# Second layer's output product in four of six token blocks: seven products of halves in place of eight for two of three output chunks

## The chip, the cores and the metric

The kernel runs on one core of one Trainium2 chip. Times are device microseconds (us) of one execution. Engines are named as the profile names them: PE is TensorE's matmuls, PEld its weight loads, DVE is VectorE, ACT is ScalarE, POOL is GpSimd, and SP is the queue that issues the DMAs.

## The reference

```python
def _attn_ref(q, k, v, beta):            # a delta-rule recurrence over 768 steps, 4 x 8 heads of 48
    ...
def _moe_ref(x, w_in, w_out):            # first layer
    h = x @ w_in
    g = np.maximum(h, 0.0) + np.log1p(np.exp(-np.abs(h)))
    return (g @ w_out).astype(np.float32)

def _moe2_ref(x, w_in, w_out):           # second layer: the change is in its g @ w_out
    h = x @ w_in
    g = h * np.cos(h)
    return (g @ w_out).astype(np.float32)

x = np.ascontiguousarray(attn_out.transpose(0, 2, 1, 3)).reshape(B * S, H * D)   # 3072 x 384
x = _moe_ref(x=x, **moe_kwargs)          # w_in 384 x 2048, w_out 2048 x 384
return _moe2_ref(x=x, **moe2_kwargs)
```

## The kernel before

The attention recurrence runs in 24 steps of 128 tokens (4 batches of 32). The first layer follows it in blocks of 256 tokens and fills PE between the recurrence's steps; the second layer runs in `NB2` = 6 blocks of 512 tokens after it, and its first blocks overlap the first layer's end. Every float32 matrix product is made of three float16 matmuls, on the high and low halves of both operands (`PAIRS`: high by high, high by low, low by high), which add up in one PSUM bank.

In the second layer (`ph` = 1) a block `j` goes through the 16 slices of 128 hidden units (`u` = `f`). `moe_in` makes the slice's h: nine matmuls (3 chunks of 128 inputs by 3 halves), each of 512 token columns, into one of five PSUM banks (psH0, psH1, psC0, psC1, psY; `hring`). Then comes a chain of operations of 128x512: on DVE an add that rounds (L918) and a subtraction (`stt`, L415), on ACT Abs and Sin (`actf`, L420 and L422), on DVE the product that gives g (L415), on ACT a copy to float16, the high half (`copy`, L399), and on POOL or DVE a subtraction that leaves the low half (`tt`, L411). `moe_out` then makes, for each of the three chunks of 128 outputs, three matmuls of 512 columns that add into that chunk's accumulator bank (accA, accB and psA; `acc2`). It comes two slices behind `moe_in`. `moe_end` copies the three accumulators to SBUF (`xs`, which lies in `w0`), and three DMAs store them.

The order of instructions is not the order of the code. Each call of `put` records an operation with the engines that it may run on, its estimated duration and the keys that it reads and writes, and `Plan.run` works out an order for each engine from these estimates. Its decisions are fixed in the built program: every engine runs its own list in order, and waits on semaphores for the others. For the `base` of a second-layer matmul the planner takes `moe_left`, the matmul time that is still to come.

Weights come as float32; `conv` splits each slice into float16 halves (`v`, one tile for two slices; L481 the high half, L489 the low half) while the first layer ends.

Of the kernel before, what the change touches and what calls it, by code (L numbers as in the profile page):

```python
# [292 lines left out]
def delta_moe_moe_kernel(ctx, tc, q, k, v, beta, mask, ident, w1, w2, out):  # L293
# [657 lines left out]
    def moe_end(ph, j):  # L951
        if ph == 0:
            av = (accA, accB[:, 0:2 * P].unsqueeze(1))
            cs = ((0, 2), (2, 3))
# [12 lines left out]
        else:
            xs = wbuf[0][0].bitcast(F32).rearrange("p o n -> p (o n)").rearrange("p (k t) -> p k t", k=KC)
            t0 = j * 4 * P
            for c, (a, key) in enumerate(acc2):  # L970
                ks = [("xs2", c)] + ([("w", 0, f, o) for f in range(2) for o in range(2)] if j == 0 else [])
# [1 line left out]
                dma(out[:, c, t0:t0 + 4 * P], xs[:, c], [("out", j, c)], [("xs2", c)], 0.73, issue=0.65)
# [156 lines left out]
```

## Time and profile before

| | us |
|---|---|
| median of 3 runs | 999.28 |
| lowest, highest | 997.36, 1003.77 |
| the profiled execution, its own time | 998.97 |
| its span, first to last instruction | 997.2 |

The median is the kernel's time. The profiled execution is one further run; 1.8 us of its time lie outside its span. Busy shares of the page are averages over the attention part, the first layer and the second layer, which have different limits. The second layer's last four blocks fill about the stretch from 744 us to 992 us of the span.

### The profile page before, as it was taken

Reading aid. Unit: us, or ns where it says so; the run is one execution under the profiler, and the core shown is the slowest. Engines: PE = TensorE matmul, PEld = TensorE weight load, DVE = VectorE, ACT = ScalarE, POOL = GpSimd, SP = SyncE. Lnnn points to the kernel's source line nnn. Section 1 sums busy time; section 2 is a strip of 40 time slices with the busy share of each in tenths; the row PEclk is TensorE's granted clock in tenths of the full one; section 3 lists DMA queues with packets and bytes.
Section 4 is the critical chain, followed back from the end, with each engine's and each line's share of the span. In section 5 each row is a group of like instructions: output and inputs, shape, how many; then the busy total and the mean of one; then the engine's idle time right before and its main releaser. Section 6 shows DMA issues by size and latency. Waiting matters only on the chain.

```text
span 997.2 us, 26273 instructions
## 1 busy us (share of the span) xinstructions
PE 947.3 (95%) x10796; PEld 672.3 (67%) x10796; DVE 675.6 (68%) x1346; ACT 685.1 (69%) x1354; POOL 355.3 (36%) x329
## 2 busy tenths in 40 slices
PE   5777989999999999999999999999999999999998
PEld 3446879988989998999898878444444444444443
DVE  8899987588668667765867654885545545455453
ACT  6575769788867878787777879766545555455554
POOL 4022236236423533453334344553223232233222
PEclk9998999999999999999999999999999999999999
DMA  6999797866875678567688722011000010000000
GB/s 210 300 285 188 173 258 164 203 159 155 162 171 130 126 162 203 105 137 171 130 219 220 160 67 96 16 64 64 1 32 32 1 64 1 32 32 0 33 1 33
DMA packets 302312, 118.71 MB, mean 119 GB/s; under 512 B 269168, under 2 KB 284784, under 8 KB 302192
## 3 DMA queue, kind: packets, MB, share of 16 engines
q1 hardware_dynamic: 302192, 117.03, 46.8%
q8 instruction: 85, 1.39, 0.6%
q14 instruction: 35, 0.29, 0.1%
HBM read 71.90 MB, written 35.65 MB: 108 GB/s over the span
## 4 chain that ended last, share of the span: by engine, by line
PE 46%; ACT 2%; DVE 1%; DMA 1%; SPq 0%; issue 0%; POOL 0%; DVEq 0%; ACTq 0%
PE psH L881 11%; PE accA L943 9%; PE accB L943 7%; PE psC L881 7%; PE psA L943 6%; PE psY L881 4%; PE psC L750 1%; DMA bdA<-kpd 1%; PE psY L750 0%; SPq L390 0%; ACT e L422 0%; ACT e L904 0%; ACT e L898 0%; DVE e L918 0%; ACT psH L909 0%; ACT g L399 0%
## 5 line engine op out<-in xcount | busy, mean ns | idle before, releaser
L411 POOL TENSOR_TENSOR g<-g,g 128x512 f16<-128x512 f32 x190 | 225.7, 1188 | 457.0 <-ACT g L399 417.9
L881 PE MATMUL psH<-xt,w 128*128 128x256 f16 x1728 | 223.4, 274 | 1.8 <-DVE g L411 1.8
L399 ACT ACTIVATE g<-g 128x512 f16<-128x512 f32 x192 | 120.6, 628 | 90.3 <-DVE g L415 63.0
L943 PEld LDWEIGHTS <-w 128*128 128x128 f16 x1728 | 162.0, 97 | 20.2 <-issue 1.6
L881 PEld LDWEIGHTS <-w 128*128 128x128 f16 x1728 | 160.4, 98 | 20.6 <-issue 2.1
L943 PE MATMUL accA<-g,w 128*128 128x256 f16 x1152 | 156.4, 272 | 0.9 <-POOL g L411 0.8
L943 PEld LDWEIGHTS <-v 128*128 128x128 f16 x864 | 84.6, 98 | 101.9
L881 PEld LDWEIGHTS <-v 128*128 128x128 f16 x864 | 84.5, 98 | 101.8 <-issue 1.3
L420 ACT ACTIVATE e<-e 128x512 f32<-128x512 f32 x96 | 60.4, 630 | 85.9 <-DVE e L415 85.6
L411 DVE TENSOR_TENSOR g<-psH,e 128x512 f32<-128x512 f32 x96 | 65.7, 685 | 44.0 <-ACT e L422 37.2
L943 PE MATMUL accB<-g,w 128*128 128x256 f16 x576 | 91.9, 272 | 0.0
L881 PE MATMUL psH<-xu,v 128*128 128x512 f16 x351 | 83.3, 379 | 0.0
L881 PE MATMUL psC<-xu,v 128*128 128x512 f16 x342 | 81.2, 379 | 0.0
L943 PE MATMUL accA<-g,v 128*128 128x512 f16 x288 | 77.8, 379 | 0.0
L943 PE MATMUL accB<-g,v 128*128 128x512 f16 x288 | 77.8, 379 | 0.0
L943 PE MATMUL psA<-g,v 128*128 128x512 f16 x288 | 77.7, 379 | 0.0
L750 PEld LDWEIGHTS <-bdA 128*128 128x128 f16 x1968 | 63.2, 98 | 18.8 <-issue 15.9
L898 ACT ACTIVATE e<-psH 128x512 f32<-128x512 f32 x95 | 56.2, 591 | 28.5 <-PE psH L881 28.0
L422 ACT ACTIVATE e<-e,hpi 128x512 f32<-128x512 f32 x96 | 69.1, 721 | 2.8
L750 PEld LDWEIGHTS <-bdKQ 128*128 128x128 f16 x1840 | 59.9, 97 | 6.9 <-issue 3.2
L422 ACT ACTIVATE e<-e 128x512 f32<-128x512 f32 x96 | 60.1, 626 | 1.0
L415 DVE SCALAR_TENSOR_TENSOR g<-psH,e 128x512 f32<-128x512 f32 x39 | 27.0, 692 | 49.7 <-ACT e L422 49.7
(169 smaller groups left out, 1543.6 us busy)
## 6 DMA issues: line engine op xcount, KB each, us to landing
bdKQ<-kqd SPq DMA_DIRECT2D x92, 128.0 KB, 4.1
kpd<-kp SPq DMA_DIRECT2D x24, 448.0 KB, 3.9
bdA<-kpd SPq DMA_DIRECT2D x96, 112.0 KB, 3.7
kqd<-kq SPq DMA_DIRECT2D x20, 512.0 KB, 4.6
raw<-w_dram SPq DMA_DIRECT2D x12, 768.0 KB, 5.3
w<-w_dram SPq DMA_DIRECT2D x10, 768.0 KB, 7.1
v<-w_dram SPq DMA_DIRECT2D x10, 768.0 KB, 5.0
qt<-q_dram SPq DMA_DIRECT2D x24, 256.0 KB, 4.2
```

What stands on the lines that cost most here:

```text
L399: nc.scalar.activation(out=out, in_=in_, func=AF.Copy, scale=scale)
L411: put(var, w, r, lambda e: eng[e].tensor_tensor(out=out, in0=a, in1=b, op=op), port=True, **kw)
L415: lambda e: nc.vector.scalar_tensor_tensor(out, in0=a, scalar=s, in1=b, op0=op0, op1=op1), port=True, **kw)
L420: nc.scalar.activation(out=out, in_=in_, func=func, scale=scale)
L422: nc.scalar.activation(out=out, in_=in_, func=func, scale=scale, bias=bias)
L750: nc.tensor.matmul(ps[:, h, 0:D], lhsT=lhs(h), rhs=mov[:, h], start=(first and i == 0 and h == 0), stop=(last and i == len(passes) - 1 and ...
L881: nc.tensor.matmul(hp[:, i] if ph == 0 else hp, lhsT=w[:, l, kc * P:(kc + 1) * P], rhs=xv[:, m * KC + kc], start=(kc == 0 and idx == 0), s ...
L898: nc.scalar.activation(out=ev, in_=hv, func=AF.Abs, scale=sc)
L943: nc.tensor.matmul(acc[c], lhsT=w[:, l, c * P:(c + 1) * P], rhs=rhs, start=(f == 0 and idx == 0 and (ph == 1 or c != 1)), stop=(f == NF - ...
```

## The change

The second layer's blocks 2 to 5 (`SEVEN`) take slices in pairs `p` = (2p, 2p+1). For output chunks 0 and 1 of a pair, the product of a 2x2 arrangement of weight pieces (two slices by two chunks, each 128x128) and a 2x2 arrangement of g pieces (two slices by two halves of 256 tokens) is made with seven products of sums of pieces where eight were before (the Strassen scheme in Winograd's form). A product is three matmuls of 256 columns. Chunk 2 stays as it was, three matmuls of 512 columns for each slice. The last pair of the last block is done without the scheme (`plain`): eight products of 256 columns.

What is new around it: `weight_sums` makes four sums of weight pieces for each of the 8 pairs, once, and splits them into float16 halves (`wsum`, in the tile `bdKQ`). `pair_in` is `moe_in` for a slice with a ring of three PSUM banks (psH0, psH1, psC0), and leaves g in float32 (`gpair`, in `bdA2`) and its halves in `pair16` (in `w8` and `w10`). `pair_sums` makes four sums of g pieces (`gsum`: one operation of 512 columns, two of 256) and splits them into halves (`sum16`: two copies and two subtractions of 512), all in `bdA2`. `pair_out` issues the products; the results add up in halves of the banks accA (products 1 and 2), accB (5 and 7), psC1 (6 and 4) and psY (3), and in psA (chunk 2). `pair_end` combines the seven sums into chunks 0 and 1 with one copy and seven additions of 256 columns (`part`, in `w2`), and stores chunk 2 first.

```diff
@@ -53,6 +53,8 @@
 LO_N = 0
 NEG = 1.0, W_SC
 NT = 2 * P, 4 * P
+SEVEN = range(2, 6)
+PLAIN = True
 Z = 72 * C
 X2 = 2 * C
 N2 = C // 2
@@ -860,7 +862,7 @@
...
-    moe_left = [4 * NF * 9 * (NB * mm(2 * P) + NB2 * mm(4 * P)) / 2]
+    moe_left = [4 * NF * 9 * (NB * mm(2 * P) + NB2 * mm(4 * P)) / 2 - len(SEVEN) * NFP * 3 * mm(2 * P)]
...
@@ -968,9 +970,164 @@
...
...
+    wsum = bdKQ.rearrange("p m s b x -> p (m s b x)").rearrange("p (f l i n) -> p f l i n", f=NFP, l=2, i=4)
+    room = bdA2.rearrange("p s b x -> p (s b x)")
+    gpair = [room[:, 2048 * i:2048 * i + 2048].bitcast(F32).rearrange("p (i t) -> p i t", i=4) for i in range(2)]
+    gsum = room[:, 4096:6144].bitcast(F32).rearrange("p (i t) -> p i t", i=4)
+    sum16 = [room[:, 6144 + 2048 * i:8192 + 2048 * i].rearrange("p (l i t) -> p l i t", l=2, i=4) for i in range(2)]
+    late = bdT.rearrange("p h b x -> p (h b x)").bitcast(F32)
+    wf, ws = late[:, 0:512].rearrange("p (f n) -> p f n", f=2), late[:, 512:].rearrange("p (i n) -> p i n", i=4)
+    pair16 = [wbuf[0][4 + i].rearrange("p o n -> p (o n)").bitcast(F16)[:, 0:2048].rearrange("p (l i t) -> p l i t", l=2, i=4) for i in range(2)]
+    part = wbuf[0][1].rearrange("p o n -> p (o n)").bitcast(F32)[:, 0:1536].rearrange("p (i t) -> p i t", i=6)
+    ring7 = [(flat[i][0], [flat[i][1]]) for i in (1, 2, 4)]
+    place = {1: (3, 0), 2: (3, 1), 5: (7, 0), 7: (7, 1), 6: (5, 0), 4: (5, 1), 3: (6, 0), 9: (6, 1)}
+    pc, spare = [0], [None]
+
+    def spot(k):
+
+        if k == 8:
+            return spare[0], 0
+        i, h = place.get(k, (0, 0))
+        return flat[i], 2 * P * h
+
+    def weight_sums():
+
+        for p in range(NFP):
+            def whole(e, p=p):
+                w = wbuf[1][p].rearrange("p f n -> p (f n)").bitcast(F16).rearrange(
+                    "p (f o l n) -> p f o l n", f=2, o=2, l=2)[:, :, 1]
+                eng[e].tensor_tensor(out=wf, in0=w[:, :, 0, 0:2 * P], in1=w[:, :, 1, 0:2 * P], op=ALU.add)
+
...
+            put([("DVE", dve(512)), ("POOL", pool(512))], [("wf",)] + own, wk, whole, port=True)
+            lo, hi = slice(0, P), slice(P, 2 * P)
+            tt(ws[:, 0], wf[:, 0, hi], wf[:, 1, hi], ALU.add, [("ws", 0)], [("wf",)], P)
+            tt(ws[:, 2], wf[:, 0, lo], wf[:, 0, hi], ALU.subtract, [("ws", 2)], [("wf",)], P)
+            tt(ws[:, 1], ws[:, 0], wf[:, 0, lo], ALU.subtract, [("ws", 1)], [("wf",), ("ws", 0)], P)
+            tt(ws[:, 3], wf[:, 1, lo], ws[:, 1], ALU.subtract, [("ws", 3)], [("wf",), ("ws", 1)], P)
+            WS = [("ws", i) for i in range(4)]
...
+            copy(wsum[:, p, 0], ws, 1.0, [("wsum", p, 0)] + own, WS + ([("wsum", 0, 0)] if p else []), 512)
+            tt(wsum[:, p, 1], ws, wsum[:, p, 0], ALU.subtract, [("wsum", p, 1)], WS + [("wsum", p, 0)], 512)
+
+    def pair_in(f, xk, x):
+        i, b = f % 2, pc[0] % 2
+        s = un[0] % 2
+        hp, hk = ring7[un[0] % 3]
+        un[0] += 1
...
+        n = 4 * P
+        ev = eb[s].rearrange("p a t -> p (a t)")
+        gv, hi, lo = (t.rearrange("p a t -> p (a t)") for t in (
+            gpair[b][:, 2 * i:2 * i + 2], pair16[b][:, 0, 2 * i:2 * i + 2], pair16[b][:, 1, 2 * i:2 * i + 2]))
...
+        mg = 1.5 * 2.0 ** 23 * U_SC
+        put([("DVE", dve(n))], ek, hk, lambda e: nc.vector.tensor_scalar_add(ev, hp, mg))
+        stt(ev, ev, mg, hp, ALU.subtract, ALU.subtract, ek, hk, n)
+        actf(ev, ev, AF.Abs, ek, [], n)
+        actf(ev, ev, AF.Sin, ek, [("hpi",)], n, scale=-2.0 * math.pi / U_SC, bias=hpi)
+        stt(gv, hp, G2_SC / U_SC, ev, ALU.mult, ALU.mult, gk + (bk("bdA") + bk("bd2") + bk("bdG") if own else []), hk + ek, n)
...
+        copy(hi, gv, 1.0, [("p16", b, i, 0)] + old, gk, n)
+        tt(lo, gv, hi, ALU.subtract, [("p16", b, i, 1)], gk + [("p16", b, i, 0)], n)
+
+    def pair_sums():
+        b = pc[0] % 2
+        g, GK = gpair[b], [("gp", b, 0), ("gp", b, 1)]
+        tt(gsum[:, 0:2], g[:, 1:4:2], g[:, 0:2], ALU.subtract, [("gs", 0)], GK, 512)
+        tt(gsum[:, 2], g[:, 3], gsum[:, 0], ALU.subtract, [("gs", 1)], GK + [("gs", 0)], 256)
+        tt(gsum[:, 3], gsum[:, 2], g[:, 2], ALU.subtract, [("gs", 2)], GK + [("gs", 1)], 256)
+        for a in range(2):
+            x, y = gsum[:, 2 * a:2 * a + 2], sum16[b][:, :, 2 * a:2 * a + 2]
+            xk = [("gs", 0)] if a == 0 else [("gs", 1), ("gs", 2)]
+            copy(y[:, 0], x, 1.0, [("s16", b, a, 0)], xk, 512)
+            tt(y[:, 1], x, y[:, 0], ALU.subtract, [("s16", b, a, 1)], xk + [("s16", b, a, 0)], 512)
+        pc[0] += 1
+        return b
+
+    def pair_out(p, b, plain=False, short=False):
+        f0, f1 = 2 * p, 2 * p + 1
+
+        def w(f, c):
+            return lambda l: wview(1, f)[:, 1][:, l, c * P:(c + 1) * P], [("w", 1, f, 0), ("w", 1, f, 1)]
+
+        def sw(i):
+            return lambda l: wsum[:, p, l, i], [("wsum", p, 0), ("wsum", p, 1)]
+
+        def bg(i):
+            return lambda m: pair16[b][:, m, i], [("p16", b, i // 2, 0), ("p16", b, i // 2, 1)]
+
+        def bs(i):
+            j = (0, 2, 1, 3)[i]
+            return lambda m: sum16[b][:, m, j], [("s16", b, j // 2, 0), ("s16", b, j // 2, 1)]
+
+        def both(i):
+            return (lambda m: pair16[b][:, m, 2 * i:2 * i + 2].rearrange("p i t -> p (i t)"),
+                    [("p16", b, i, 0), ("p16", b, i, 1)])
+
+        if plain:
+            todo = [(k, w(f, c), bg(2 * i + t)) for i, f in ((0, f0), (1, f1)) for k, c, t in ((2, 0, 0), (3, 0, 1), (8, 1, 0), (9, 1, 1))]
+            todo = todo[:4] + [(0, w(f0, 2), both(0)), (0, w(f1, 2), both(1))] + todo[4:]
+        else:
+            todo = [(1, w(f0, 0), bg(0)), (2, w(f1, 0), bg(2)), (0, w(f0, 2), both(0)), (0, w(f1, 2), both(1)),
+                    (5, sw(0), bs(0)), (7, sw(2), bs(2)), (6, sw(1), bs(1)), (3, sw(3), bg(3)), (4, w(f1, 1), bs(3))]
+        for q, (k, (lhs, lk), (rhs, rk)) in enumerate(todo):
+            bank, col0 = spot(k)
+            at = slice(col0, col0 + (4 * P if k == 0 else 2 * P))
...
+            us = 3 * mm(at.stop - at.start)
+            moe_left[0] -= us
+            put([("PE", us)], [bank[1]], lk + rk, fn, base=moe_left[0])
+
+    def pair_end(j, plain=False):
+        xs = wbuf[0][0].bitcast(F32).rearrange("p o n -> p (o n)").rearrange("p (k t) -> p k t", k=KC)
+        t0, n = j * 4 * P, 2 * P
+        sc = 2.0 * math.pi / (G2_SC * W_SC)
+
+        def add(out, w, k, u, sign=1.0):
+            bank, col0 = spot(k)
+            stt(out, bank[0][:, col0:col0 + n], sign * sc, part[:, u], ALU.mult, ALU.add, [w], [bank[1], ("part", u)], n)
+
...
+        copy(part[:, 0], flat[place[1][0]][0][:, 0:n], sc, [("part", 0)] + (own if j == SEVEN[0] else []), [flat[place[1][0]][1]], n, ps=True)
+        add(part[:, 1], ("part", 1), 6, 0)
+        add(part[:, 2], ("part", 2), 5, 1)
+        add(part[:, 3], ("part", 3), 7, 1)
+        left = [(xs[:, 0, 0:n], ("xs2", 0, 0), 2, 0), (xs[:, 0, n:], ("xs2", 0, 1), 3, 2)]
+        if plain:
+            add(part[:, 4], ("part", 4), 4, 3, -1.0)
+            add(part[:, 5], ("part", 5), 5, 3)
+            left += [(xs[:, 1, 0:n], ("xs2", 1, 0), 8, 4), (xs[:, 1, n:], ("xs2", 1, 1), 9, 5)]
+        else:
+            left += [(xs[:, 1, n:], ("xs2", 1, 1), 5, 3), (xs[:, 1, 0:n], ("xs2", 1, 0), 4, 3, -1.0)]
+        for x in left:
+            add(*x)
+        copy(xs[:, 2], flat[0][0], sc, [("xs2", 2, 0), ("xs2", 2, 1)], [flat[0][1]], 4 * P, ps=True)
+        for c in (2, 0, 1):
+            dma(out[:, c, t0:t0 + 4 * P], xs[:, c], [("out", j, c)], [("xs2", c, 0), ("xs2", c, 1)], 0.73, issue=0.65)
 
...
+        if ph and j in SEVEN:
+            was, plain = None, PLAIN and j == NB2 - 1
+            for p in range(NFP):
+                for i in range(2):
+                    pair_in(2 * p + i, xk, x)
+                if plain and p == NFP - 1:
+                    spare[0] = flat[(1, 2, 4)[un[0] % 3]]
+                    b = pc[0] % 2
+                else:
+                    b = pair_sums()
+                if p:
+                    pair_out(p - 1, was, short=plain)
+                was = b
+            pair_out(NFP - 1, was, plain)
+            return pair_end(j, plain)
...
@@ -1060,6 +1232,7 @@
...
+    weight_sums()
     for j in range(NB2):
         moe_block(1, j)
```

Up to the middle of the second layer's first two blocks all engines' lists are as before. From there to the end PE has 384 matmuls of 512 columns fewer and 675 of 256 columns more (in blocks 2 to 5). The lists differ most in these two places.

On POOL, in the last blocks. Before, its list there holds only the low halves of g, one for each slice (`g16` from `g`):

```order
L411 TENSOR_TENSOR g160_97<-g1_94,g160_97 128x512
L411 TENSOR_TENSOR g161_98<-g0_93,g161_98 128x512
L411 TENSOR_TENSOR g162_99<-g1_94,g162_99 128x512
L411 TENSOR_TENSOR g160_97<-g0_93,g160_97 128x512
L411 TENSOR_TENSOR g161_98<-g1_94,g161_98 128x512
```

Changed, in the last pairs that are summed: `w8` and `w10` receive the low halves of g, and the rows `bdA2<-bdA2` are the sums (512, then two of 256) and the low halves of the sums (512):

```order
L413 TENSOR_TENSOR w10_84<-bdA2_102,w10_84 128x512
L413 TENSOR_TENSOR bdA2_102<-bdA2_102 128x512
L413 TENSOR_TENSOR bdA2_102<-bdA2_102 128x256 x2
L413 TENSOR_TENSOR bdA2_102<-bdA2_102 128x512
L413 TENSOR_TENSOR w8_83<-bdA2_102,w8_83 128x512
```

So all the new sums of g stand on POOL, between the low halves that were there before: seven operations for a pair where two were. The copies to high halves stand on ACT.

At the end of the program, on DVE. Before, the last row there is the last slice's g, and ACT's list ends with the three copies of the accumulators to `w0`:

```order
L918 TENSOR_SCALAR e0_95<-psH0_140 128x512
L415 SCALAR_TENSOR_TENSOR e0_95<-e0_95,psH0_140 128x512
L415 SCALAR_TENSOR_TENSOR g1_94<-psY_147,e1_96 128x512
L918 TENSOR_SCALAR e1_96<-psH1_141 128x512
L415 SCALAR_TENSOR_TENSOR e1_96<-e1_96,psH1_141 128x512
L415 SCALAR_TENSOR_TENSOR g0_93<-psH0_140,e0_95 128x512
L415 SCALAR_TENSOR_TENSOR g1_94<-psH1_141,e1_96 128x512
```

Changed, the last slice's g is followed by the additions of `pair_end` (`w2` is `part`, `w0` the stored result):

```order
L417 SCALAR_TENSOR_TENSOR bdA2_102<-psC0_145,e1_96 128x512
L417 SCALAR_TENSOR_TENSOR w0_79<-accA_142,w2_80 128x256
L417 SCALAR_TENSOR_TENSOR w2_80<-psC1_146,w2_80 128x256
L417 SCALAR_TENSOR_TENSOR w2_80<-accB_143,w2_80 128x256 x2
L417 SCALAR_TENSOR_TENSOR w0_79<-psY_147,w2_80 128x256
L417 SCALAR_TENSOR_TENSOR w2_80<-psC1_146,w2_80 128x256
L417 SCALAR_TENSOR_TENSOR w2_80<-accB_143,w2_80 128x256
L417 SCALAR_TENSOR_TENSOR w0_79<-psH0_140,w2_80 128x256
L417 SCALAR_TENSOR_TENSOR w0_79<-psY_147,w2_80 128x256
```

Nine additions now stand behind the last g, on banks that PE's last matmuls write (accB, psY, psH0).

## Rows read from the trace of the kernel before

**Rows 1.** Busy time of the whole span, and PE and its granted clock in 40 slices.
```profile
PE 947.3 (95%) x10796; PEld 672.3 (67%) x10796; DVE 675.6 (68%) x1346; ACT 685.1 (69%) x1354; POOL 355.3 (36%) x329
...
PE   5777989999999999999999999999999999999998
...
PEclk9998999999999999999999999999999999999999
```

**Rows 2.** Windows: length, busy time and count of each engine, granted clock, DMA.
```profile
640.00:744.00 104.00, 104.00 (x483) 47.15 (x482) 63.80 (x91) 60.17 (x92) 40.68 (x33) 1.00 0.11 39
...
744.00:992.00 248.00, 248.00 (x1150) 112.45 (x1149) 130.97 (x192) 132.84 (x206) 74.02 (x64) 1.00 0.05 20
```

**Rows 3.** Chain that ended last, 585 to 600 us: start, time, what.
```profile
591.13 3.93 PE psH L881 x36
595.06 1.94 PE psY L881 x9
```

**Rows 4.** The page's groups: the first layer's weight loads.
```profile
L943 PEld LDWEIGHTS <-w 128*128 128x128 f16 x1728 | 162.0, 97 | 20.2 <-issue 1.6
```

**Rows 5.** POOL's subtractions by tile (g, kp, v): ns min/median/max, first and last start.
```profile
L411 POOL TENSOR_TENSOR g<-g,g x190: 1152/1158/1947, 113.2 to 987.9; 128x512 f16<-128x512 f32 x190
...
L411 POOL TENSOR_TENSOR kp<-kt,kp x40: 722/736/1323, 14.0 to 434.3; 128x256 f16<-128x256 f32 x40
...
L489 POOL TENSOR_TENSOR v<-cv,v x16: 1641/1647/2361, 521.7 to 674.4; 128x768 f16<-128x768 f32 x16
```

**Rows 6.** Timeline: two of POOL's subtractions back to back.
```profile
986.75 2.27 POOL L411 TENSOR_TENSOR g<-g,g 128x512 f16<-128x512 f32 x2 [1.57 <-ACT g L399]
```

**Rows 7.** Timeline in block 5, one slice on its way to halves (start, time).
```profile
971.49 0.69 DVE L918 TENSOR_SCALAR e<-psC 128x512 f32<-128x512 f32 x1 [0.26 <-PE psC L881]
...
972.22 0.69 DVE L415 SCALAR_TENSOR_TENSOR e<-e,psC 128x512 f32<-128x512 f32 x1
...
972.94 0.63 ACT L420 ACTIVATE e<-e 128x512 f32<-128x512 f32 x1 [0.98 <-DVE e L415]
...
973.60 0.72 ACT L422 ACTIVATE e<-e,hpi 128x512 f32<-128x512 f32 x1
974.42 0.69 DVE L415 SCALAR_TENSOR_TENSOR g<-psC,e 128x512 f32<-128x512 f32 x1 [1.52 <-ACT e L422]
...
975.21 0.63 ACT L399 ACTIVATE g<-g 128x512 f16<-128x512 f32 x1 [0.89 <-DVE g L415]
...
975.92 1.16 POOL L411 TENSOR_TENSOR g<-g,g 128x512 f16<-128x512 f32 x1 [2.72 <-ACT g L399]
```

**Rows 8.** Timeline at a block's end: a low half, and the output matmuls behind it.
```profile
929.30 1.15 POOL L411 TENSOR_TENSOR g<-g,g 128x512 f16<-128x512 f32 x1 [3.07 <-ACT g L399]
...
931.15 0.81 PE L943 MATMUL accA<-g,v 128*128 128x512 f16 x3
```

**Rows 9.** Chain that ended last, its end: start, time, what.
```profile
991.53 1.31 PE psA L943 x6
992.84 0.02 issue
992.86 0.60 ACT w L399
```

**Rows 10.** Timeline of DVE: operations of 384 and of 512 columns on a PSUM bank.
```profile
578.22 0.55 DVE L415 SCALAR_TENSOR_TENSOR y<-psY,y 128x384 f16<-128x384 f32 x1
...
984.05 0.69 DVE L415 SCALAR_TENSOR_TENSOR e<-e,psH 128x512 f32<-128x512 f32 x1
984.66 0.69 DVE L415 SCALAR_TENSOR_TENSOR g<-psH,e 128x512 f32<-128x512 f32 x1
```

**Rows 11.** Timeline: a POOL subtraction that starts beside one of DVE's weight conversions.
```profile
580.97 0.95 DVE L468 SCALAR_TENSOR_TENSOR cv<-v,cv 128x768 int32<-128x768 int32 x1
...
581.01 1.93 POOL L411 TENSOR_TENSOR g<-g,g 128x512 f16<-128x512 f32 x1 [3.13 <-ACT g L399]
```

**Rows 12.** POOL's groups from 690 to 992 us: busy, mean ns, idle before.
```profile
L411 POOL TENSOR_TENSOR g<-g,g 128x512 f16<-128x512 f32 x79 | 91.4, 1157 | 211.1 <-ACT g L399 211.1
```

More of the change, by code (lines that the diff above doesn't have):

```diff
@@ L970, in moe_end @@
             for c, (a, key) in enumerate(acc2):
[L971 removed]
+                ks = [("xs2", c, 0), ("xs2", c, 1)] + ([("w", 0, f, o) for f in range(2) for o in range(2)] if j == 0 else [])
                 copy(xs[:, c], a, 2.0 * math.pi / (G2_SC * W_SC), ks, [key], 4 * P, ps=True)
[L973 removed]
+                dma(out[:, c, t0:t0 + 4 * P], xs[:, c], [("out", j, c)], [("xs2", c, 0), ("xs2", c, 1)], 0.73, issue=0.65)
@@ new lines, in pair_in, with fn @@
+    def pair_in(f, xk, x):
[3 more added lines that the diff above has]
+        un[0] += 1
+        for kc in range(KC):
+            def fn(e, kc=kc):
+                w, xv = wview(1, f)[:, 0], x()
+                for idx, (l, m) in enumerate(PAIRS):
+                    nc.tensor.matmul(hp, lhsT=w[:, l, kc * P:(kc + 1) * P], rhs=xv[:, m * KC + kc],
+                                     start=(kc == 0 and idx == 0), stop=(kc == KC - 1 and idx == 2))
+            us = 3 * mm(NT[1])
+            moe_left[0] -= us
+            put([("PE", us)], hk, xk + [("w", 1, f, 0)], fn, base=moe_left[0])
+        n = 4 * P
+        ev = eb[s].rearrange("p a t -> p (a t)")
+        gv, hi, lo = (t.rearrange("p a t -> p (a t)") for t in (
+            gpair[b][:, 2 * i:2 * i + 2], pair16[b][:, 0, 2 * i:2 * i + 2], pair16[b][:, 1, 2 * i:2 * i + 2]))
+        ek, gk = [("e", s)], [("gp", b, i)]
+        own = pc[0] < 2
+        mg = 1.5 * 2.0 ** 23 * U_SC
[4 more added lines that the diff above has]
+        stt(gv, hp, G2_SC / U_SC, ev, ALU.mult, ALU.mult, gk + (bk("bdA") + bk("bd2") + bk("bdG") if own else []), hk + ek, n)
+        old = [(x, 0, f0, o) for x in ("w",) for f0 in (8 + 2 * b, 9 + 2 * b) for o in range(2)] if own else []
+        old += [("wl", f0, o) for f0 in (8 + 2 * b, 9 + 2 * b) for o in range(2)] if own else []
+        copy(hi, gv, 1.0, [("p16", b, i, 0)] + old, gk, n)
+        tt(lo, gv, hi, ALU.subtract, [("p16", b, i, 1)], gk + [("p16", b, i, 0)], n)
@@ new lines, in pair_out, with fn @@
+    def pair_out(p, b, plain=False, short=False):
[22 more added lines that the diff above has]
+            if plain:
+                head, tail = k == 8 and q < 4, q >= (6 if k else 5) and k != 3
+            else:
+                head = p == 0 and (k in (1, 5, 6, 3) or q == 2)
+                tail = k in (7, 4) if short and p == NFP - 2 else p == NFP - 1 and (k in (2, 7, 4, 3) or q == 3)
+            def fn(e, bank=bank, at=at, lhs=lhs, rhs=rhs, head=head, tail=tail):
+                for idx, (l, m) in enumerate(PAIRS):
+                    nc.tensor.matmul(bank[0][:, at], lhsT=lhs(l), rhs=rhs(m), start=(idx == 0 and head), stop=(idx == 2 and tail))
+            us = 3 * mm(at.stop - at.start)
+            moe_left[0] -= us
+            put([("PE", us)], [bank[1]], lk + rk, fn, base=moe_left[0])
@@ new lines, in pair_end @@
+    def pair_end(j, plain=False):
[5 more added lines that the diff above has]
+            stt(out, bank[0][:, col0:col0 + n], sign * sc, part[:, u], ALU.mult, ALU.add, [w], [bank[1], ("part", u)], n)
+        own = [("w", 0, f, o) for f in range(2, 4) for o in range(2)] + [("wl", f, o) for f in range(2, 4) for o in range(2)]
+        copy(part[:, 0], flat[place[1][0]][0][:, 0:n], sc, [("part", 0)] + (own if j == SEVEN[0] else []), [flat[place[1][0]][1]], n, ps=True)
[3 more added lines that the diff above has]
+        left = [(xs[:, 0, 0:n], ("xs2", 0, 0), 2, 0), (xs[:, 0, n:], ("xs2", 0, 1), 3, 2)]
+        if plain:
+            add(part[:, 4], ("part", 4), 4, 3, -1.0)
[7 more added lines that the diff above has]
+        for c in (2, 0, 1):
+            dma(out[:, c, t0:t0 + 4 * P], xs[:, c], [("out", j, c)], [("xs2", c, 0), ("xs2", c, 1)], 0.73, issue=0.65)
```

4 lines of the change are left out of this document (added).

## The prediction, made before the changed kernel was run

> **What bounds the kernel now.** I read busy time and clock first, then the windows of the second layer, then the chain that ended last. PE is busy 95% of the span, and in the last 30 of the 40 slices it stands at nine tenths or more [rows 1]. In the windows of the second layer PE fills every microsecond, 248.00 of 248.00 us in blocks 2 to 5, at a granted clock of 1.00, the 2.4 GHz level, while DVE has 131, ACT 133 and POOL 74 us of work [rows 2]. So in the stretch that the change touches, the time is the number of matmuls times their spacing, and the other engines have room: of a slice's period they use 53%, 54% and 30%. The spacing stands in the chain: 36 matmuls of 256 columns in 3.93 us are 0.1092 us each, 9 of 512 columns in 1.94 us are 0.2156 us each [rows 3]. Halving the columns nearly halves the time, since the weight load of 0.097 us [rows 4] still fits behind a matmul of 0.109 us. Two matmuls of half the columns cost 0.003 us more than the whole one.
>
> **PE, removed and added.** A pair had 36 matmuls of 512 columns: 36 x 0.2156 = 7.76 us. It now has 24 of 512 (18 for h, 6 for chunk 2) and 7 x 3 = 21 of 256: 5.17 + 2.29 = 7.47 us. That is 0.294 us less for each of the 31 pairs that are summed. The plain pair has 24 x 0.1092 in place of 12 x 0.2156, 0.03 us more. From the order's counts: 384 x 0.2156 - 675 x 0.1092 = 82.79 - 73.71 = 9.08 us. It all lies on the path that sets the end, if PE stays full. It is also the most that the change can bring.
>
> **The sums of g on POOL.** The new operations stand on POOL and ACT. For a pair POOL has five operations of 512 columns and two of 256. A 512 takes 1.158 us [rows 5], the second of two in a row adds 2.27 - 1.16 = 1.11 us [rows 6]. A plain 256 isn't in the trace. The rows for 512 and 768 columns (1.158 and 1.647) give 0.489 us for 256 columns, so a 256 would be 0.67 us; the nearest row itself, 256 columns in another layout, has 0.736 [rows 5]. POOL's work for a pair is then between 5 x 1.11 + 2 x 0.67 = 6.89 us and 5 x 1.16 + 2 x 0.736 = 7.27 us, 92% to 97% of PE's 7.47 us. I take the lower end, since the operands are plain rows as those of the 512 are. POOL is nearly full, and no longer an idle engine. ACT has for a pair two each of 0.63, 0.72 and 0.63 us and two new copies of 0.63 us, 5.22 us in all; DVE keeps six of 0.61 to 0.69 us, 4.1 us at most [rows 7]. Both have cover.
>
> **Whether the sums come in time.** From the end of a slice's h, DVE and ACT need 3.62 us to g (971.49 to 975.11), ACT's high half another 0.73, POOL's low half 1.24 [rows 7]. In the order POOL then makes the first sum (1.11), ACT its high half (0.73, with POOL's next sum beside it), POOL its low half (1.24). From a low half's end to the matmuls on it 0.70 us were enough without a wait of PE (930.45 to 931.15) [rows 8]. Together 9.37 us. In the changed order the work that PE has between the last matmul of a pair's h and the first on that pair's sums (accB) is 11.05 us at the least among 31 pairs, counted with the two spacings: 1.7 us to spare. For the second half of the sums (psC1) POOL adds a 256 (0.67) and two 512 (2.22): 12.26 us against at least 13.0 us. So I expect hardly any wait in the steady state. With 0.7 us the thinner place bears little disturbance, and I put 0.7 us on waits in all (0 to 6 us: six is 0.2 us at every pair).
>
> **Edges.** The weight sums (on POOL but for one on DVE, their copies on ACT) run beside blocks 0 and 1. POOL's longest run there between two low halves of g is, with the next low half, three of 512 and two of 128 columns, 3 x 1.11 + 2 x 0.42 = 4.17 us (0.42 by the same line), and the run behind it 3.06 us, against 2 x 3.88 us of PE work for two slices; PE's distance from h to its use is 7.76 us there, 1.3 us over the 6.47 us that the slice whose low half stands in the rows had without a wait [rows 8]. I cost them at nothing; without that cover each would cost some 0.3 us, 2 us in all. Between blocks the accumulators must be read before the next block writes them; the shortest distance in the order is psY's, 1.95 us of PE work against one addition of 0.41 us, so nothing again. The three DMAs of a block stay; chunk 2's now comes first.
>
> **The end.** Before, ACT's copy of 0.60 us closed the last matmul [rows 9], 0.62 us behind it. Now the last nine additions stand on DVE, and seven of them must wait for accB's last matmul, which nine matmuls of 256 columns follow (0.98 us). An addition of 256 columns from PSUM isn't in the trace: 0.55 us for 384 and 0.69 us for 512 columns give 0.41 us, and in a row a 512 adds 0.61 us, so a 256 some 0.34; one that needs the one before adds 0.12 more (0.73 us from 971.49 to 972.22) [rows 7, 10]. Six steps of 0.34 to 0.46 and a last of 0.41 us end 1.5 to 2.2 us behind the last matmul: 0.9 to 1.6 us later than before. I take 1.25 us, as about half of them depend on the one before.
>
> **Sum.** -9.08 + 1.25 + 0.7 = -7.1 us. Against the profiled execution's 998.97 us that is 991.9 us; the median of the runs is 0.3 us above that execution, so I say 992.0 us, 0.7% less.
>
> **A rule weighed.** Where POOL starts beside a DVE operation with two SBUF inputs, its 512 columns take 1.93 us in place of 1.16 [rows 11]. In blocks 2 to 5, where every DVE operation reads PSUM, the mean of 79 is 1.157 us [rows 12]. The Trainium skill (SBUF — State Buffer, section "Who interferes with whom") says the same of the chip: a DVE instruction with at most one SBUF input, outside the two-port modes, does not contend with GpSimd, and otherwise the loser blocks fully. By that rule the new additions on DVE, which read a PSUM bank and one SBUF operand, leave POOL alone. The skill (GPSIMD Engine Reference, section "4.1 Engine selection") also speaks against the change: it keeps elementwise work on VectorE, with GpSimd about 2x slower. Here it is 1.158 to 0.69 us. If PE is full this costs nothing; if POOL is not in time it is the second rival below.
>
> **Rivals.** First, thin waits: PE stands for 0.1 to 0.3 us at each of 32 pairs, because POOL's queue, in order and 92% to 97% full, has to wait for ACT's copies in between, and what it loses it regains at only 0.2 to 0.6 us a pair. For it: ACT's list also holds Abs and Sin of later slices ahead of such a copy. Against it: 1.7 and 0.7 us to spare. It gives 3 to 10 us, so 994 to 1001 us.
>
> Second, on the other side: POOL sets the pace. It decides from the point where POOL's pair passes PE's 7.47 us; from there each 0.1 us a pair costs 3.2 us. With the stretched 1.93 us [rows 11] for two of its five operations, and 1.11 and 0.67 us for the rest, a pair takes 3.86 + 3.33 + 1.34 = 8.53 us, 1.06 us over: 32 x 1.06 = 34 us, 991 + 34 = 1025 us. With 0.56 us over it is 1% slower (1009 us). For it: the load, and 1.947 us as the longest 512 in the trace [rows 5]. Against it: the 79 even ones, and that nothing in these blocks makes DVE read two SBUF operands.
>
> Third, everything is hidden and the end costs 0.9 us: 998.97 - 9.08 + 0.9 = 990.8 us. To be faster by over 1% the median would have to fall below 989.3 us, beyond what the sum can give; only the spread of the runs (997.36 to 1003.77) brings it there. That the change doesn't do what it says can be left aside: the order shows the 384 and 675 matmuls.
>
> **Chances.** Forecast and third rival together, 989 to 994 us: 0.70, of which I give 0.10 to a time under 989.3 us. Thin waits, 994 to 1001 us: 0.20. POOL in the lead: 0.10, nearly all of it over 1009 us. About 1% is what a measurement of this kernel can tell from no change. Faster by over 1% then has 0.10, within 1% 0.81, slower by over 1% 0.09. The range goes from 988.5 us, the full 9.08 us less the smaller end and a run's spread, to 1000 us, most of the thin waits.
>
> **What would show it.** Right: between the first summed pair and the end PE is busy without gaps at clock 1.00, a summed pair passes every 7.47 us (four blocks in some 239 us where 248 were), POOL is busy over 90% there with 512s of 1.16 us, and from the last matmul to the end of the last addition 1.5 to 2.2 us pass. Thin waits: PE's gaps before accB or psC1 matmuls with POOL as releaser, short and at every pair. POOL in the lead: POOL without idle time, its 512s or 256s longer than here. Wrong from the start I would be if 256-column matmuls with ever new weights from four tiles kept a larger spacing than 0.109 us, or if blocks 0 and 1 lost time to the weight sums.

## The result, and the profile of the changed kernel

The changed kernel took 990.6 us (median of 4 runs, 987.08 to 993.99), the kernel before 999.83 us beside it (4 runs, 997.36 to 1003.77): ratio 0.9897, 95% interval 0.9869 to 0.9926. Later, beside the second group of experiments (six runs against eleven), it took 988.12 us against 998.02: ratio 0.9908 (0.9884 to 0.9933). The forecast was 992.0 us in a range from 988.5 to 1000.

The profiled execution of the changed kernel took 987.08 us with a span of 985.3, that of before 998.97 with 997.2. These 11.9 us are not all the change's. The product that starts the second layer is the same instruction in both, and PE's order ahead of it is the same. Here it is in the timelines (start, length, engine, line, operation, count) of four executions, with the span of each. The kernel before, and the kernel before once more (run e10 below):

```profile
core 0 of [0], span 997.2 us
...
585.12 2.10 PE L881 MATMUL psC<-xu,v 128*128 128x512 f16 x9
```

```profile
core 0 of [0], span 992.0 us
...
579.91 2.11 PE L881 MATMUL psC<-xu,v 128*128 128x512 f16 x9
```

The changed kernel, and the changed kernel once more (run e5):

```profile
core 0 of [0], span 985.3 us
...
581.07 2.11 PE L883 MATMUL psC<-xu,v 128*128 128x512 f16 x9
```

```profile
core 0 of [0], span 983.2 us
...
578.97 2.11 PE L883 MATMUL psC<-xu,v 128*128 128x512 f16 x9
```

The start moves by several us between executions of one kernel. From it to the end of the span it is 412.08 and 412.09 us before, 404.23 and 404.23 us after. So in these executions the change is worth 7.85 us from there on, and two executions of a kernel agree on that within the 0.1 us to which a span is printed. It is the yardstick of the experiments below, called the stretch.

Windows of the changed kernel (length, then busy time and count of PE, its weight loads, DVE, ACT, POOL, then the granted clock, the DMA share, GB/s), blocks 0 and 1 and then about the last four, as in [rows 2]:

```profile
core 0: us, PE busy (x) PEld busy (x) DVE busy (x) ACT busy (x) POOL busy (x), PEclk, DMA share, GB/s
640.00:744.00 104.00, 104.00 (x484) 47.16 (x482) 64.12 (x92) 63.62 (x99) 69.24 (x78) 1.00 0.11 39
...
740.00:800.00 60.00, 60.00 (x352) 34.33 (x351) 32.21 (x49) 39.50 (x66) 53.77 (x53) 1.00 0.08 27
800.00:860.00 60.00, 60.00 (x363) 35.33 (x361) 34.53 (x56) 39.50 (x66) 56.84 (x56) 1.00 0.08 27
860.00:920.00 60.00, 59.80 (x363) 35.32 (x361) 34.57 (x56) 39.59 (x66) 56.24 (x56) 1.00 0.04 14
920.00:980.00 60.00, 59.80 (x370) 35.93 (x368) 34.11 (x57) 40.68 (x68) 56.72 (x56) 1.00 0.04 14
```

PE is as full as before, at the same clock of 1.00 (2.4 GHz), with more and shorter matmuls. POOL went from 30% to 93%. What PE waited for from 640 us on is the whole of this list (engine and line, what it waited for, us in total, times, longest):

```profile
PE psC L1100 <- POOL bdA L413: 0.2, 1, 0.2
PE accA L1100 <- POOL w L413: 0.2, 1, 0.2
```

The list counts from the modelled end of a matmul. By the starts of its matmuls PE lost a little more, as is worked out below.

POOL's groups from 735 to 986 us, different shapes apart (busy and mean ns, idle time before them and its releaser), answer to [rows 5, 12]:

```profile
L413 POOL TENSOR_TENSOR w<-bdA,w 128x512 f16<-128x512 f32 x64 | 73.7, 1159 | 7.6 <-ACT w L401 7.6
L413 POOL TENSOR_TENSOR bdA<-bdA 128x512 f16<-128x512 f32 x62 | 71.5, 1159 | 5.3 <-ACT bdA L401 5.3
L413 POOL TENSOR_TENSOR bdA<-bdA 128x256 f32<-128x256 f32 x62 | 45.3, 730 | 3.0
L413 POOL TENSOR_TENSOR bdA<-bdA 128x512 f32<-128x512 f32 x31 | 39.5, 1274 | 0.9 <-DVE bdA L417 0.9
```

The first row is the low halves of g, the second those of the sums, then the two sums of 256 columns and the first sum of 512. The end in the timeline answers to [rows 6, 9, 10]:

```profile
977.00 0.27 PE L1100 MATMUL psC<-bdA,bdKQ 128*128 128x256 f16 x1
977.47 0.38 PE L1100 MATMUL psC<-bdA,bdKQ 128*128 128x256 f16 x2 [0.20 <-POOL bdA L413]
...
978.66 0.82 PE L1100 MATMUL accB<-bdA,bdKQ 128*128 128x256 f16 x6
...
979.32 0.49 PE L1100 MATMUL psY<-w,v 128*128 128x256 f16 x3
...
979.52 0.76 DVE L417 SCALAR_TENSOR_TENSOR w<-accB,w 128x256 f32<-128x256 f32 x2 [0.88 <-PE accB L1100]
979.64 0.82 PE L1100 MATMUL psH<-w,v 128*128 128x256 f16 x6
980.19 0.41 DVE L417 SCALAR_TENSOR_TENSOR w<-psY,w 128x256 f32<-128x256 f32 x1
...
981.18 0.41 DVE L417 SCALAR_TENSOR_TENSOR w<-psH,w 128x256 f32<-128x256 f32 x1
981.51 0.41 DVE L417 SCALAR_TENSOR_TENSOR w<-psY,w 128x256 f32<-128x256 f32 x1
```

The last six matmuls start at 979.64 and end at 980.46, counted as the end of 992.84 us before was in [rows 9]; the last addition ends at 981.92, 1.46 us behind them.

### The profile page after: what moved, and what is told of

Its sections match the earlier page's. It is cut to its first block, busy times and chain, and to the rows that moved or that the text cites. A ratio compares the mean times of both kernels' runs of the same rounds, so it can differ in the third digit from the quotient of the medians.

```text
span 985.3 us, 27228 instructions
## 1 busy us (share of the span) xinstructions
PE 938.2 (95%) x11087; PEld 701.8 (71%) x11087; DVE 684.2 (69%) x1377; ACT 714.8 (73%) x1420; POOL 535.3 (54%) x531
## 5 line engine op out<-in xcount | busy, mean ns | idle before, releaser
L413 POOL TENSOR_TENSOR g<-g,g 128x512 f16<-128x512 f32 x126 | 152.3, 1209 | 245.5 <-ACT g L401 216.1
L413 POOL TENSOR_TENSOR bdA<-bdA 128x512 f16<-128x512 f32 (+2 forms) x155 | 154.1, 1010 | 9.2 <-ACT bdA L401 5.3
L401 ACT ACTIVATE g<-g 128x512 f16<-128x512 f32 x128 | 80.4, 628 | 37.1 <-DVE g L413 20.8
L422 ACT ACTIVATE e<-e 128x512 f32<-128x512 f32 x96 | 60.0, 625 | 57.0 <-DVE e L417 56.3
L1027 PEld LDWEIGHTS <-v 128*128 128x128 f16 x576 | 56.4, 98 | 53.8
L1027 PE MATMUL psH<-xu,v 128*128 128x512 f16 x378 | 91.2, 379 | 0.0
L413 POOL TENSOR_TENSOR w<-bdA,w 128x512 f16<-128x512 f32 x64 | 73.7, 1159 | 7.6 <-ACT w L401 7.6
L1100 PEld LDWEIGHTS <-v 128*128 128x128 f16 x495 | 48.4, 98 | 23.0 <-issue 0.4
L401 ACT ACTIVATE bdA<-bdA 128x512 f16<-128x512 f32 x62 | 38.9, 627 | 33.5 <-POOL bdA L413 32.7
L424 ACT ACTIVATE e<-e 128x512 f32<-128x512 f32 x96 | 60.1, 626 | 1.0
L906 ACT ACTIVATE e<-e 128x512 f32<-128x512 f32 x96 | 59.8, 623 | 0.1
L911 ACT ACTIVATE psH<-psH 128x512 f32<-128x512 f32 x96 | 57.2, 596 | 0.0
```

The costliest lines, as they stand in the source:

```text
L401: nc.scalar.activation(out=out, in_=in_, func=AF.Copy, scale=scale)
L422: nc.scalar.activation(out=out, in_=in_, func=func, scale=scale)
L424: nc.scalar.activation(out=out, in_=in_, func=func, scale=scale, bias=bias)
L906: put([("ACT", act(n))], ek, [], lambda e: nc.scalar.activation(out=ev, in_=ev, func=AF.Exp, scale=-1.0 if how[0] == "ACT" else -sc))
L911: nc.scalar.activation(out=hv, in_=hv, func=AF.Relu, scale=sc)
L1027: nc.tensor.matmul(hp, lhsT=w[:, l, kc * P:(kc + 1) * P], rhs=xv[:, m * KC + kc], start=(kc == 0 and idx == 0), stop=(kc == KC - 1 and idx ...
```

## The experiments

The theory: PE's matmuls set the time, the change takes its 9 us from them, POOL delivers the sums just in time and has some 6% left, and the end gives a little back. Rivals: POOL already takes part of the gain; the weight sums beside blocks 0 and 1 cost something; or part of the gain has nothing to do with the products. Stretches and ratios of all runs (each ratio against the kernel before on the same chip):

| run | seven products in | stretch, us | ratio (95%) |
|---|---|---|---|
| before, before again (e10) | none | 412.08, 412.09 | |
| e1 | none, weight sums kept | 411.7 | 1.0004 (0.9986 to 1.0022) |
| e7 | blocks 4, 5 | 408.6 | 0.9952 (0.9939 to 0.9966) |
| the change, e5 | blocks 2 to 5 | 404.23, 404.23 | 0.9897, 0.9908 |
| e9, first sum from one piece | blocks 2 to 5 | 404.2 | one run |
| e6, sums in the last pair too | blocks 2 to 5 | 406.2 | 0.9945 (0.9929 to 0.9960) |
| e3, sums of g on DVE | blocks 2 to 5 | 408.8 | 0.9948 (0.9926 to 0.9970) |
| e4, one more 512 on POOL a pair | blocks 2 to 5 | 425.6 | 1.0126 (1.0099 to 1.0153) |
| e2 | blocks 1 to 5 | 421.1 | 1.0083 (1.0062 to 1.0104) |
| e8, as e2, weight sums on DVE | blocks 1 to 5 | 406.8 | 0.9918 (0.9903 to 0.9933) |

In e2 and e8 the planner puts the first product of the second layer ahead of 18 of the first layer's matmuls of 256 columns. Their stretches hold 18 x 0.109 = 2.0 us more work by that, so beside the others they are 419.1 and 404.8 us.

**e1, the weight sums alone.**

```diff
-SEVEN = range(2, 6)
+SEVEN = range(6, 6)
```

> The eight weight sums are made, but no block uses them (the output product stays as before in all six blocks). Theory (the gain is PE's shorter work, and the sums lie beside it): from the first second-layer matmul to the end of the span the kernel takes what the one before took, 412.1 us, within 0.5 us, and its ratio to the kernel before is 1.000. Rival (the changed program's first part got faster as such, by some 4 us as in the two profiles, by its different later part): the ratio is 0.996, with the first second-layer matmul near 581 us in place of 585.

Measured: 999.01 us, ratio 1.0004. POOL has the sums in its windows and PE lost nothing (window of 700 to 720 us):

```profile
700.00:720.00 20.00, 20.00 (x95) 9.07 (x93) 10.55 (x16) 11.88 (x19) 19.35 (x27) 1.00 0.01 1
```

POOL works 19.35 of 20 us, PE stays at 20.00. The weight sums are free here, and nothing in this run says that the part ahead of the second layer got faster by the changed program: this execution reached the second layer at 588.23 us, the latest of all.

**e2, one block more.**

```diff
-SEVEN = range(2, 6)
+SEVEN = range(1, 6)
```

> The scheme in five blocks in place of four. Theory: PE's work shrinks by another 8 x 0.294 = 2.35 us and the sums stay hidden; from the first second-layer matmul to the end 404.2 - 2.35 = 401.9 us, 988 us in all, ratio to the kernel before 0.987. Rival (POOL is at its limit and the weight sums, now squeezed into block 0 beside the weight conversions, come late): PE waits by several us before block 1's sums, and the stretch is 404 us or more.

Measured: 1006.06 us, ratio 1.0083. My theory of a further gain fell, the rival held. Windows of block 1:

```profile
700.00:720.00 20.00, 20.00 (x120) 11.51 (x119) 11.55 (x17) 12.79 (x22) 19.84 (x22) 1.00 0.00 1
720.00:740.00 20.00, 16.57 (x94) 8.80 (x92) 9.48 (x14) 11.76 (x20) 20.00 (x25) 1.00 0.11 40
740.00:760.00 20.00, 17.56 (x87) 9.49 (x88) 6.53 (x10) 10.86 (x18) 20.00 (x23) 0.83 0.00 1
760.00:780.00 20.00, 16.46 (x98) 9.37 (x97) 10.23 (x19) 11.05 (x20) 19.84 (x23) 1.00 0.10 39
```

POOL has no idle time, and PE stands: 10.8 us between 680 and 800 us. After the 3.4 us that PE stood from 720 to 740 us, the granted clock of the next window is 0.83, so part of that ran at the lower level of 1.2 GHz. In block 1 the weight sums (1.16 + 4 x 0.456 + 1.16 = 4.1 us a pair), the conversions of the last weights and the sums of g all stand in POOL's queue, and each pair's matmuls may start only when that pair's weight sums are made.

**e8, the same with the weight sums on DVE.** The edit, for all six operations of a pair's weight sums:

```diff
-            tt(ws[:, 0], wf[:, 0, hi], wf[:, 1, hi], ALU.add, [("ws", 0)], [("wf",)], P)
+            tt(ws[:, 0], wf[:, 0, hi], wf[:, 1, hi], ALU.add, [("ws", 0)], [("wf",)], P, only=("DVE",))
...
```

> The seven products in blocks 1 to 5 again, with the additions of the weight sums on VectorE alone; on GpSimd they took some 4.2 us for each of eight pairs (34 us) while block 1 ran. Theory: in block 1 GpSimd was short of time, so with these 34 us gone TensorE's waits between 680 and 800 us fall from 10 us to under 4, the granted clock stays at 1.00, and the time is 988 to 996 us, 10 us or more below the 1006 of the first form. Rival: the sums come too late because the converted weights come too late, whatever engine adds them: waits stay above 8 us on the sums, and the time stays at 1000 to 1007 us.

Measured: 989.87 us, 16 us below e2. The same windows:

```profile
700.00:720.00 20.00, 20.00 (x122) 11.73 (x120) 19.19 (x30) 14.21 (x23) 19.60 (x18) 1.00 0.00 0
720.00:740.00 20.00, 18.34 (x107) 10.11 (x106) 18.32 (x26) 12.52 (x21) 19.74 (x19) 1.00 0.13 40
740.00:760.00 20.00, 19.03 (x117) 11.41 (x118) 17.49 (x29) 13.38 (x24) 18.81 (x18) 1.00 0.11 40
760.00:780.00 20.00, 20.00 (x121) 11.55 (x120) 9.89 (x15) 12.79 (x22) 19.77 (x21) 1.00 0.01 2
```

PE stands 2.6 us between 680 and 800 us instead of 10.8, and the clock stays at 1.00. So POOL's load was e2's trouble, not late weights. But POOL is still nearly full there and DVE now too, and what a fifth block could give (8 pairs of 0.294 us, 2.35 us) is lost in these gaps: 404.8 us on the common yardstick for 404.23, and 989.87 us beside 988.12 for the changed kernel on the same chip. It is no better version.

**e3, the three sums of g on DVE.**

```diff
-        tt(gsum[:, 0:2], g[:, 1:4:2], g[:, 0:2], ALU.subtract, [("gs", 0)], GK, 512)
+        tt(gsum[:, 0:2], g[:, 1:4:2], g[:, 0:2], ALU.subtract, [("gs", 0)], GK, 512, only=("DVE",))
...
```

> The three additions that make the sums of g run on DVE in place of POOL. Theory: POOL falls from 93% to some 60% busy in blocks 2 to 5, DVE rises to some 80%, and the time stays within 1 us of the changed kernel's stretch of 404.2 us, since PE waited for POOL by only 0.4 us. DVE's 512 and 256 have two SBUF inputs, so POOL's operations beside them become longer than 1.16 us (1.3 us in the mean). Rival (POOL's load does hold PE back): the stretch gets shorter by more than 1 us. Second rival (the two engines shut each other out of SBUF so often that PE waits): longer by more than 3 us.

Measured: 992.9 us, the stretch 4.6 us longer. My theory of the same time fell, and the second rival held. PE waited 2.9 us for the sums' low halves by the list, in three waits of some 1 us, one block apart; the list leaves out stands of 0.1 to 0.2 us at other pairs. DVE's groups from 750 to 980 us, and a piece of the timeline:

```profile
L413 DVE TENSOR_TENSOR bdA<-bdA 128x256 f32<-128x256 f32 x62 | 65.6, 1059 | 1.5
...
L413 DVE TENSOR_TENSOR bdA<-bdA 128x512 f32<-128x512 f32 x31 | 22.7, 734 | 2.5
```

```profile
863.00 1.16 POOL L413 TENSOR_TENSOR w<-bdA,w 128x512 f16<-128x512 f32 x1 [0.92 <-ACT w L401]
863.49 2.25 DVE L413 TENSOR_TENSOR bdA<-bdA 128x256 f32<-128x256 f32 x2
864.12 1.33 POOL L413 TENSOR_TENSOR bdA<-bdA 128x512 f16<-128x512 f32 x1
```

A sum of 256 columns takes DVE 1.06 us on average, longer than the 0.73 us of 512 columns: two of them last 2.25 us here while POOL runs at their side. DVE's additions of 256 columns with one operand in PSUM take 0.41 us beside the same POOL. This agrees with the Trainium skill (SBUF — State Buffer, "Who interferes with whom"): a DVE instruction with two SBUF inputs contends with a GpSimd instruction that reads SBUF. POOL's own mean rose from 1.159 to 1.249 us for the sums' low halves. So although POOL's busy time falls to 36 to 38 of 60 us, the sums come later; DVE, busy 54 to 56 of 60 us from 800 us on, is now the full one.

**e4, one more operation on POOL.** Per pair an addition of 512 columns whose result nobody reads, all of POOL's operations bound to it:

```diff
...
+        dump = late[:, 0:512].rearrange("p (i t) -> p i t", i=2)
+        tt(dump, gsum[:, 0:2], g[:, 0:2], ALU.add, [("wf",)], GK + [("gs", 0)], 512, only=("POOL",))
```

> One more addition of 512 columns for each pair on POOL, its result not used, and the low halves bound to POOL. POOL's work for a pair becomes 7.1 + 1.12 = 8.2 us where PE has 7.47 us. Theory (POOL had 0.3 us a pair to spare and decides from 7.47 us): PE waits 0.7 to 0.8 us at each of 31 pairs, 22 to 25 us in all; from the first second-layer matmul to the end 426 to 430 us; ratio to the kernel before 1.014 to 1.018. Rival (POOL is far from deciding, the waits are covered by buffers): under 5 us more, ratio under 0.997.

Measured: 1010.51 us, stretch 425.6, 21.4 us or 0.69 us a pair more, just under the 22 to 25 us of the theory. Two windows, the added operation of two pairs in a row, and the largest waits of PE:

```profile
740.00:800.00 60.00, 59.45 (x346) 33.67 (x345) 32.45 (x48) 39.02 (x66) 59.90 (x58) 1.00 0.08 27
...
860.00:920.00 60.00, 56.90 (x333) 32.19 (x331) 30.06 (x49) 37.35 (x61) 60.00 (x60) 1.00 0.04 14
```

```profile
861.74 1.34 POOL L413 TENSOR_TENSOR bdT<-bdA 128x512 f32<-128x512 f32 x1
...
870.02 1.36 POOL L413 TENSOR_TENSOR bdT<-bdA 128x512 f32<-128x512 f32 x1
```

```profile
PE psH L1027 <- DVE bdA L417: 6.7, 11, 1.8
PE psC L1027 <- DVE bdA L417: 2.8, 5, 0.7
```

POOL is busy 60.00 of 60 us, and a pair takes it 8.28 us (861.74 to 870.02), 0.81 over PE's 7.47. Now POOL sets the pace, but not at once: PE is busy 59.45 us in the first window and 56.90 in the later one, so what lies ready between the engines covers the first pairs. PE's largest waits name DVE and h's bank, not POOL. The next link stands in DVE's groups from 750 to 980 us, at the operation that writes g:

```profile
L417 DVE SCALAR_TENSOR_TENSOR bdA<-psH,e 128x512 f32<-128x512 f32 x39 | 26.4, 688 | 60.4 <-POOL bdT L413 37.6 <-ACT e L424 22.7
```

DVE may not write the next g until POOL's added operation (bdT) has read the old one, and so h's bank stays full. A queue that falls behind shows up two steps away.

**e5, the change again,** with e6 to e8 on its chip:

> The changed kernel as it is, once more, so that the others of this group have it on the same chip. Theory: of the 11.9 us between the two profiled spans only 7.9 came from the change (from the first product of the second layer to the end, 404.2 us for 412.1); the 4.0 us ahead of that are spread between executions. Then that stretch is again 404 to 405 us, while its start lies anywhere between 580 and 588 us, and the ratio is 0.989 to 0.993. Rival: the part ahead of it is faster by the change too. Then it starts at 581 again, within 0.5 us, and the ratio is 0.988 or less.

Measured: 988.12 us, ratio 0.9908, stretch 404.23: the theory. Only its start, 578.97, lies 1 us below the forecast 580 to 588.

**e6, sums in the last pair too.**

```diff
-PLAIN = True
+PLAIN = False
```

> The last pair of the last block is computed by the seven products too, where the changed kernel computes it by eight. Theory: TensorE does one product of three matmuls less (0.33 us), but the last slice's result must then pass through three sums, a copy and a low half on GpSimd and ScalarE (1.27 + 0.73 + 0.73 + 0.63 + 1.16 = 4.5 us) ahead of the products that wait for it, where the eight need a copy and a low half (0.63 + 1.16 = 1.8 us): TensorE waits 1.5 to 3 us at the end, and the time is 1 to 3 us above the changed kernel's. Rival: the products of the pair before fill the wait, and the time is the same within 0.5 us or up to 0.3 us less.

Measured: 991.83 us, stretch 2.0 us longer. The waits come where GpSimd has the sums ahead of the last low halves of g:

```profile
978.27 1.15 POOL L413 TENSOR_TENSOR w<-bdA,w 128x512 f16<-128x512 f32 x1
979.38 0.73 POOL L413 TENSOR_TENSOR bdA<-bdA 128x256 f32<-128x256 f32 x1
979.48 0.38 PE L1100 MATMUL accA<-w,v 128*128 128x256 f16 x2 [1.10 <-POOL w L413]
...
981.27 0.38 PE L1100 MATMUL accA<-w,v 128*128 128x256 f16 x2 [0.66 <-POOL w L413]
```

So the plain last pair is worth 2 us: at the end nothing is left to put beside POOL's queue.

**e7, blocks 4 and 5 alone.**

```diff
-SEVEN = range(2, 6)
+SEVEN = range(4, 6)
```

> The seven products in blocks 4 and 5 alone, where the changed kernel has them in 2 to 5. Theory: each block gives 2.1 to 2.3 us on TensorE and the longer end takes 0.65 us once: two blocks are worth 3.5 to 4 us, the stretch from the second layer's first product to the end is 408 to 408.8 us, the ratio 0.996 (0.994 to 0.998). Rival: GpSimd, 93% busy beside the seven products, takes part of the gain in each block, so that two blocks give under 2.5 us, with a wait of TensorE on GpSimd in each.

Measured: ratio 0.9952, stretch 408.58: 3.50 us for two blocks and the end, 4.35 us for the other two. The rival fell. What follows the last matmul is not equally long in both, so for one block the last matmul says more. In e7:

```profile
986.23 0.82 PE L1100 MATMUL psH<-w,v 128*128 128x256 f16 x6
...
987.87 0.41 DVE L417 SCALAR_TENSOR_TENSOR w<-psY,w 128x256 f32<-128x256 f32 x1
```

From the first product (583.42) to the last matmul's end (987.05) it is 403.63 us, in the change 399.39 (581.07 to 980.46): 4.24 us for blocks 2 and 3, 2.12 us each. From 640 us on PE waited once, 0.2 us by the list. So POOL's load takes little from each block's gain.

**e9, the first sum from one piece.**

```diff
-        tt(gsum[:, 0:2], g[:, 1:4:2], g[:, 0:2], ALU.subtract, [("gs", 0)], GK, 512)
+        tt(gsum[:, 0:2], g[:, 2:4], g[:, 0:2], ALU.subtract, [("gs", 0)], GK, 512)
```

> The first of the three sums of slices, which took GpSimd 1.274 us where the low halves of the same 128x512 take 1.159 us, reads two separate halves as its first operand. Here it reads one piece instead (another pair of slices, so that this sum is not the one the reference needs); type and size stay. Theory: the 32-bit operands and result are what costs, since 128, 256 and 512 columns of them took 0.45, 0.73 and 1.274 us, which lies on one line; then it still takes 1.26 to 1.28 us. Rival: the separated halves cost it; then it takes 1.14 to 1.18 us. TensorE's part is the same either way: 404.2 us, within 0.4, from the second layer's first product to the end.

Measured, in POOL's groups from 735 to 987 us:

```profile
L413 POOL TENSOR_TENSOR bdA<-bdA 128x512 f32<-128x512 f32 x31 | 39.5, 1274 | 0.9 <-DVE bdA L417 0.9
```

The same 1.274 us: not the separated halves.

**e10, before again.** No edit.

> The kernel before, once more, for where its second layer starts. Theory: the start moves between executions of one kernel (585.1 us in its first profiled execution), by several us, while the stretch from there to the end stays at 412.1 within 0.4 us. Rival: the kernel before always starts there at 585, within 1 us, and the changed one earlier.

Measured: start at 579.91, stretch 412.09, 993.77 us in a single run. The start of one and the same kernel moved by 5.2 us.

## Why the prediction was right

**PE's 9.08 us, and 0.7 us of waits.** Right. From the first product of the second layer to the last matmul's end it is 407.72 us before (585.12 to 992.84) and 399.39 after (581.07 to 980.46), 8.33 us less where 9.08 - 0.7 = 8.38 were forecast. PE stood in three places. At 977.00 a matmul of 256 columns and the next start 0.47 us apart in place of 0.11, which costs 0.36 us and not the 0.2 of the list; at 897.53 it is the same, and at 922.58 it is 0.15 us, which the list leaves out. Together 0.87 us, so the matmuls alone give 9.2 us. Per block it is 2.12 us (e7 against the change), with half of the 0.5 us by which the change stands longer than e7 added 2.38, where eight pairs of 0.294 make 2.35. The feared larger spacing of matmuls with ever new weights didn't come: the six of 256 columns at 978.66 us are 0.66 us ahead of the next group, 0.11 us each. The margin of the sums was real but thin: e6 and e2 show what comes when a little more is put into POOL's queue.

**POOL per pair.** Right, within the bounds of 6.89 to 7.27 us: POOL is busy 169.8 of the 180 us from 800 to 980, 24.1 pairs of 7.47 us, so 7.05 us a pair. The value taken, the lower end, was too low by 0.16 us, and most of that is the first sum, taken as one of the 512s, which takes 1.274 us where they take 1.159. The 256 columns took 0.730 us, near the upper of the two values. None of it reached the time, since it stayed under 7.47 us.

**Weight sums and edges at nothing.** Right (e1), as long as the sums have two blocks' time. With one block (e2) they cost more than all blocks give.

**The end, 1.25 us.** Too much. The last addition ended 1.46 us behind the last matmul, at the lower end of the 1.5 to 2.2 us of the forecast, and 0.84 us later than ACT's copy did before (0.62). The seven additions behind accB's last matmul follow each other at 0.33 us (979.52 to 981.51 in six steps). I had given about half of them 0.12 us more, as if they needed the one just before; by the code each of them takes a `part` that was made at least two additions earlier. From the last addition to the span's end it is 3.38 us where it was 3.74 (993.46 to 997.2), so that the end costs 0.84 - 0.36 = 0.48 us. That 0.36 us is not the work of the new end: e7, which has the same end, takes 3.7 us there (988.28 to 992.0), and e1, which has the old one, only 3.3 (its copy ends at 996.58 of 999.9). What decides it was not tried.

**Sum.** -8.33 + 0.48 = -7.85 us where -8.38 + 1.25 = -7.1 were forecast. Nearly all of the difference of 0.7 us is the end, half of it by the steps of the additions and half by the 0.36 us behind them, which the forecast did not have.

**The second rival** didn't come, since POOL stayed at 7.05 us a pair; that POOL sets the pace once it is past 7.47 is what e4 shows at 8.28 us. Where between the two it begins was not sought. The rule of 3.2 us for each 0.1 us gives 26 us for 0.81 us over, and 21.4 were measured: the first pairs are covered. The rival asked for stretched POOL operations, and there were none (the low halves of the sums take 1.159 us); e3, whose sums read two SBUF operands on DVE, has them at 1.249 us. The rule that elementwise work belongs on VectorE (the Trainium skill, GPSIMD Engine Reference, "4.1 Engine selection"), followed here for the three sums of g, costs 4.6 us of stretch, though DVE's 512 columns take 0.73 us and POOL's 1.27.

**What stays open.** The ratios of the change, of e5, e7 and e3 are 1.3 to 2.4 us better than their stretches say (0.9908 is 9.2 us of 998.02, the stretch 7.85), that of e6 0.4 us worse. The median of 990.6 us is 1.4 us under the 992.0 that the stretch alone makes of the 999.83 beside it. The intervals reach 1.3 to 2.9 us to either side, and the start moves by more than that between executions, so this may be chance; that the part ahead of the second layer gains a microsecond is not shown and not excluded. It decides on which side of a gain of 1% the change lies.

## What to carry to other kernels

Replacing products by sums paid most of the matmul time that fell away (8.3 of 9.2 us) while the engine with the sums stayed under the matmul time of one step (7.05 of 7.47 us); work that out per step, not per kernel. At 0.8 us beyond, the kernel lost 0.69 us a step, most of it. Where the sums of constant operands are made matters as much: they need a stretch in which that engine is free. To judge changes of under 1%, look for an instruction that both kernels share, just ahead of the change, and measure from there: here the whole time spreads by 7 us and that stretch by less than 0.1. Look whether the order ahead of it is the same, as it is not in e2 and e8.

## What the hardware showed that was not expected

POOL's operations of two tensors with 32-bit operands and results took 0.456 (128 columns), 0.730 (256) and 1.274 us (512), while the 512 columns with 16-bit operands took 1.155 to 1.159 us, whether these were both inputs or one input and the result; a first operand in two separated pieces cost nothing (e9). DVE's sum of 256 columns from SBUF took longer (1.06 us) than that of 512 (0.73 us), with POOL's operations beside it (e3).
